# Decode attention: the K cache loaded in two transfers of 64 partitions, 32 KB to a partition

## The chip, the core and the metric

The kernel runs on one core of a Trainium2 chip. The metric is the device time of one execution in microseconds, the median of several runs. The core's engines are named as in the profile: PE (TensorE, matrix products), PEld (its weight loads), DVE (VectorE), ACT (ScalarE), POOL (GpSimd) and SP (SyncE, which issues most transfers here). Transfers between the chip's main memory and the core's on-chip memory run on 16 DMA engines. On-chip tiles have up to 128 partitions; a matmul's result goes to an accumulator memory (tiles with names in `_ps`).

## What is computed

One decode step for 8 sequences (B = 8, one token each, D = 512): attention over the last W = 2048 cached positions with 32 query heads on 8 cached heads (rep = 4) of Dh = 128, times the silu of a gated unit (F = 1792), added to x:

```python
xn = layernorm(x)
q = xn @ wq                                        # 32 heads of 128
k, v = the last 2048 positions of the caches       # 8 heads
p = softmax(q k^T * Dh**-0.5)
s = (p v) @ wo
h = sigmoid(xn @ w_gate) * (xn @ w_up)
out = x + s * silu(h @ w_down)
```

All inputs are bfloat16. The caches' windows are 33.55 MB each for K and V, wq and wo 4.19 MB each, gate, up and down 1.84 MB each: 81 MB that are read once.

## The kernel before, in words

**Loads.** Large tiles go through a ring of RING = 5 buffers of 128 partitions x 32 KB (`ring_tile`, L86). The list `loads` (L156) fixes their order: wq, K0, K1, K2, V0, then K3 V1, K4 V2, ... K7 V5, then V6, V7, gate and up, down, wo. `issue_loads` (L164) issues the next loads whenever a buffer is free (`free_bufs`); SP issues them all, in that order, on one queue. A buffer is free when its scores (`qk`, for a K) or its sums (`pv`, for a V) are done. A load's issue also waits until an earlier transfer that used the same one of eight completion semaphores has landed. Beside these, ACT loads x (`x_bf`, L84), and `load_x2` (L121) makes the copy of x that the last sum needs, x2, of two halves: POOL copies the first, and SP loads the second, 4 KB, between V1 and K4.

**Where K and V lie.** `load_heads` (L105) makes one transfer for a batch of K or V: each partition receives VC = 64 consecutive positions of two cached heads, that is two runs of 16 KB; partition 4p + gl holds positions 64p to 64p + 63 of the heads 2 gl and 2 gl + 1. The second index of the two is called gg.

**Setup.** POOL and DVE make constant tiles from an identity (L178 to L306), among them: SumM and Jneg, which spread the maximum over a group of rows and multiply it by the scale; Hm and quarter, masks over partitions; Cm4 and Cm2, masks for the sums; spr, for the spread; qz0 and qz1, zeroed here and filled with each batch's q by ACT. q is projected by PE (L316) when wq has landed.

**The loop over batches** (L614 to L652) is ordered by hand. In iteration b the DVE turns K of batch b in place, in blocks of 32 x 32 words (`k_turn`, four pieces n = 0 to 3 of 128 x 2048 words, L384), and between the pieces come the steps of the softmax for batch s = b - 1 and the sums for batch b - 3: `soft_max_part` (maximum of a row, L414, and a matmul with SumM, L420), `pv_rows` (L538), `soft_exp` (L424: one ACT exp that also sums), `soft_spread` (L438: a DVE transpose to pt_bf, 16 matmuls of 128 columns with spr to pc_ps, an ACT copy to pc_bf), `soft_den_part`, `soft_mask` (L475: four DVE multiplications by the columns of Hm that make pT). Then PE makes the scores of batch b in `qk` (L386): 32 matmuls of 32 output partitions x 512 columns into s_ps, for each of four words `we`, two gg and four gl. The half gg of the K tile lies in the pieces 2 gg and 2 gg + 1, so the matmuls of gg = 0 need only the first two pieces. Then PE makes `pv` (L491) of batch b - 2, 16 or 32 matmuls for each gg from pT and the V tile.

**The tail.** After the loop: `pv` and `pv_rows` for the last batches, the gated unit (`unit_in` to u_ps, L569; `unit_mid`, which makes hT; `unit_out` to b_ps, L599, and the gate), and 128 small matmuls with wo into a_ps (L676), which follow wo's pieces as they land. Two DVE operations on the result (prod, L690, and y, L694, which adds x2) and two stores end the kernel.

Of the kernel before, what the change touches and what calls it, by code (L numbers as in the profile page):

```python
# [10 lines left out]
def kernel(  # L11
# [13 lines left out]
    nc = tc.nc  # L25
    P = 128
    B, _, D = A_x.shape
    _, Hkv, Sk, Dh = A_k_cache.shape
    Hq = A_wq.shape[1] // Dh
    rep = Hq // Hkv  # L30
# [15 lines left out]
    NC16 = 16  # L46
    CL = VC // NC16
    GR = GL * rep
# [55 lines left out]

    def load_heads(t, cache, b):  # L105
        nc.sync.dma_start(
            out=t[:],
            in_=cache[b, :, win0:Sk, :].rearrange("h (p c) d -> p h (c d)", c=VC),
        )

    def load_k(b):
        t = ring_tile("k_sb")
        k_tiles[b] = t
        load_heads(t, A_k_cache, b)

    def load_v(b):
        t = ring_tile("v_sb")
        v_tiles[b] = t
        load_heads(t, A_v_cache, b)

    def load_x2():  # L121
        nc.gpsimd.tensor_copy(out=x2_sb[:B, :], in_=x_bf[:, :DC])
        nc.sync.dma_start(
            out=x2_sb[32 : 32 + B, :], in_=A_x.flatten_outer_dims()[:, DC:]
        )

# [30 lines left out]
    for b in range(3, B):  # L157
        loads += [(load_k, b), (load_v, b - 2)]
        if b == 3:
            loads.append((load_x2,))  # L160
    loads += [(load_v, B - 2), (load_v, B - 1), (load_in,), (load_down,), (load_wo,)]
    free_bufs = [RING]

    def issue_loads():  # L164
        while loads:
            small_one = loads[0][0] is load_x2
            if not small_one and free_bufs[0] == 0:
                return
            f, *a = loads.pop(0)
            f(*a)  # L170
            if not small_one:
                free_bufs[0] -= 1

    issue_loads()

    ident = consts.tile([P, P], bf16, name="ident")  # L178
    make_identity(nc, ident[:])
# [6 lines left out]
    nc.vector.bn_aggr(out=mv[:], in_=stats[:])  # L186
    eps_t = small.tile([B, 1], f32, name="eps_t")
    nc.vector.memset(eps_t[:], 1e-5)
    rstd = small.tile([B, 1], f32, name="rstd")
# [14 lines left out]
    for kt in range(KT):  # L204
        nc.tensor.transpose(
            out=xnT_ps[:, kt, :], in_=xn_bf[:B, kt::KT], identity=ident[:B, :B]
        )
    xnT_sb = work.tile([P, KT, PW], bf16, name="xnT_sb")
    nc.vector.memzero(xnT_sb[:])
    nc.vector.tensor_copy(out=xnT_sb[:, :, :B], in_=xnT_ps[:])  # L210
# [9 lines left out]
    for gg in range(NG):  # L220
# [9 lines left out]
        rows128.append(t)  # L230
    block = consts.tile([P, QP, PW], f32, name="block")
    quarter = consts.tile([P, QP], f32, name="quarter")
    nc.vector.tensor_reduce(
# [3 lines left out]
        op=ALU.add,  # L237
    )
    nc.gpsimd.tensor_copy(
        out=block[:], in_=quarter[:].unsqueeze(2).to_broadcast([P, QP, PW])  # L240
# [8 lines left out]
    SumM = consts.tile([P, P], f32, name="SumM")  # L249
    nc.vector.tensor_copy(  # L250
        out=SumM[:].rearrange("p (g j r) -> p g j r", j=QP, r=rep),
# [4 lines left out]
    )  # L256
    Jneg = consts.tile([P, QP], f32, name="Jneg")
    nc.vector.tensor_reduce(
        out=Jneg[:],
        in_=ident[:].rearrange("p (a j r) -> p j a r", j=QP, r=rep),  # L260
        axis=AX.XY,
        op=ALU.add,
    )
    nc.vector.tensor_scalar(
        out=Jneg[:], in0=Jneg[:], scalar1=-scale, scalar2=None, op0=ALU.mult
    )
    Hm = consts.tile([P, GL], f32, name="Hm")
    nc.vector.tensor_reduce(
        out=Hm[:],
        in_=ident[:].rearrange("p (a gl) -> p gl a", gl=GL),  # L270
        axis=AX.X,
        op=ALU.add,
# [8 lines left out]
    Cm2 = consts.tile([P, 2], f32, name="Cm2")  # L281
    nc.vector.tensor_reduce(
        out=Cm2[:],
        in_=ident[:].rearrange("p (u c x) -> p c u x", c=2, x=GR),
        axis=AX.XY,
        op=ALU.add,
    )
# [3 lines left out]
    )  # L291
    spr = consts.tile([P, CL, PW // GL, GL], bf16, name="spr")
    nc.gpsimd.tensor_copy(
        out=spr[:],
        in_=ident[:].rearrange("k (gl cl p) -> k cl p gl", gl=GL, cl=CL),
    )
    quad = consts.tile([P, QP, QP, PW], bf16, name="quad")
    for a in range(QP):
# [57 lines left out]
    def q_fill(b):  # L356
        z = qz[b % 2]
        for a in range(QP):
            rows = slice(PW * a, PW * (a + 1))
            for gg in range(NG):  # L360
                c0 = gg * QP * rep + rep * a
                nc.scalar.copy(  # L362
                    out=z[rows, GL * gg : GL * (gg + 1), :, c0 : c0 + rep],
                    in_=qc_sb[rows, :, gg, :, :, b].rearrange("p gl r we -> p gl we r"),
                )
# [20 lines left out]
    def qk(b):  # L386
        s_tiles[b] = psum.tile([P, W // QP], f32, name="s_ps")
        kv = k_tiles[b][:].rearrange(
            "p (g cl c wb i gl e) -> p g gl wb e c cl i",
            g=NG,  # L390
            cl=CL,
            c=NC16,
            wb=2,
            i=PH,
            gl=GL,
        )
        for we in range(WE):
            for gg in range(NG):
                for gl in range(GL):
                    h = GL * gg + gl  # L400
                    nc.tensor.matmul(  # L401
                        s_tiles[b][PW * gl : PW * (gl + 1), :],
                        lhsT=qz[b % 2][:, h, we, :],
                        rhs=kv[:, gg, gl, we // 2, we % 2],
                        start=(we == 0 and gg == 0),
                        stop=(we == WE - 1 and gg == NG - 1),
                        tile_position=(0, PW * gl),
                        skip_group_check=True,
                    )
        k_tiles.pop(b)  # L410

    def soft_max_part(b):
        mx = small.tile([P, 1], f32, name="mx")
        nc.vector.reduce_max(out=mx[:], in_=s_tiles[b][:], axis=AX.X)  # L414
        mj = small.tile([P, QP], f32, name="mj")
        nc.vector.tensor_scalar(
            out=mj[:], in0=Jneg[:], scalar1=mx[:], scalar2=None, op0=ALU.mult
        )
        mb_ps = psum1.tile([P, QP], f32, name="mb_ps", tag="misc")
        nc.tensor.matmul(mb_ps[:], lhsT=SumM[:], rhs=mj[:], start=True, stop=True)  # L420
        return mb_ps
# [16 lines left out]
    def soft_spread(b):  # L438
        p_bf = e_tiles[b][0]
        pt_bf = ppool.tile([P, NC16, NG, QP, rep], bf16, name="pt_bf")  # L440
        nc.vector.transpose(  # L441
            out=pt_bf[:].rearrange("p c g a r -> p (c g a r)"), in_=p_bf[:]
        )
        pc_ps = psum1.tile([P, CL, NC16, NG, rep], f32, name="pc_ps", tag="pc_ps")
        for cl in range(CL):
            for a in range(QP):
                nc.tensor.matmul(  # L447
                    pc_ps[PW * a : PW * (a + 1), cl],
                    lhsT=spr[:, cl].rearrange("k p gl -> k (p gl)"),
                    rhs=pt_bf[:, :, :, a, :],  # L450
                    start=True,
                    stop=True,
                    tile_position=(0, PW * a),
                    skip_group_check=True,
                )
        pc_bf = ppool.tile([P, VC, NG, rep], bf16, name="pc_bf")
        nc.scalar.copy(  # L457
            out=pc_bf[:].rearrange("p c g r -> p (c g r)"),
            in_=pc_ps[:].rearrange("p l c g r -> p (l c g r)"),
        )  # L460
        pc_tiles[b] = pc_bf
# [13 lines left out]
    def soft_mask(b, den_ps):  # L475
        rden = small.tile([P, 1], f32, name="rden", bufs=3)
        nc.vector.reciprocal(out=rden[:], in_=den_ps[:])
        rden_tiles[b] = rden
        pc = pc_tiles.pop(b)
        pT = ppool.tile([P, NG, VC, GL, rep], bf16, name="pT_sb")  # L480
        pT_tiles[b] = pT
        for gl in range(GL):
            nc.vector.tensor_scalar(  # L483
                out=pT[:, :, :, gl, :],
                in0=pc[:].rearrange("p c g r -> p g c r"),
                scalar1=Hm[:, gl : gl + 1],
                scalar2=None,
                op0=ALU.mult,
            )

    def pv(b, gg):  # L491
# [7 lines left out]
        for m in range(VC // nch):  # L499
            cg = m % ncg  # L500
            nc.tensor.matmul(  # L501
                o_ps[rows * cg : rows * (cg + 1), :],
                lhsT=pT_tiles[b][:, gg, nch * m : nch * (m + 1)].rearrange(
                    "p c g r -> p (c g r)"
                ),
                rhs=v[:, cols * m : cols * (m + 1)],
                start=(m < ncg),
                stop=(m >= VC // nch - ncg),
                tile_position=(0, rows * cg),
                skip_group_check=True,  # L510
            )
# [218 lines left out]
```

## Time and profile before

| | |
|---|---|
| median of 3 runs | 197.66 us (197.5 to 235.91) |
| profiled execution, time | 197.44 us |
| its span, first to last instruction | 195.7 us |
| PE busy | 111.6 us (57%) |
| DVE busy | 117.6 us (60%) |
| ACT busy | 38.6 us (20%) |
| POOL busy | 6.4 us (3%) |
| mean transfer rate over the span | 415 GB/s |
| mean granted PE clock | 0.813 of full speed |

How to read the profile's lines below. The page shows the span in 40 equal slices of 4.9 us: a digit is a busy share in tenths, GB/s is what the DMA engines moved, PEclk the granted clock. A line of a window has the window and its length, then busy time and number of instructions for PE, PEld, DVE, ACT and POOL, then granted clock, the mean busy share of the 16 DMA engines, and GB/s. A line of the transfers has the tile and its source, the issuing queue, how many, KB each and the median time in us from issue to landing. A line of the timeline has start and length in us, engine, line, operation, output <- inputs, shapes, count, and in brackets how long the engine sat idle before and what ended that.

### The profile page before, as it was taken

The page shows a single profiled execution, that of the slowest core. Times are in us where ns is not written, and L with a number is a line of the kernel's source. Part 1 is how long each engine was busy: PE and PEld are TensorE (multiplying, and loading weights), DVE is VectorE, ACT ScalarE, POOL GpSimd, SP SyncE. Part 2 cuts the span into 40 slices and gives each one's busy share as a digit, 9 for nine tenths or more (in the row PEclk, how much of TensorE's full clock was granted, in tenths as well). Part 3 has the DMA queues.
Part 4 walks back from the last instruction along what each step waited for, and adds up shares of the span by engine and source line. Part 5 has one row for each costly group of instructions (what it writes and reads, how often), then busy time and mean ns, then how long its engine had stood idle before and what let it go on. Part 6 is the DMA issues. An engine that isn't in the chain of part 4 may idle for free.

```text
span 195.7 us, 2620 instructions
## 1 busy us (share of the span) xinstructions
PE 111.6 (57%) x1092; PEld 44.6 (23%) x1092; DVE 117.6 (60%) x176; ACT 38.6 (20%) x112; POOL 6.4 (3%) x22
## 2 busy tenths in 40 slices
PE   0133025709809980799059914990796199684362
PEld 0011001102002240214022411150215024462351
DVE  3404498299299449935895489739936952455001
ACT  3001910015015011501141104211501110233000
POOL 2730000000000000000000000000000000000000
PEclk9999555966985996589757985699589669999998
DMA  6999999999999999999999999999999999999991
GB/s 241 457 408 442 432 429 429 429 432 425 429 429 429 427 429 429 432 424 439 432 439 422 439 435 435 429 432 425 432 429 429 425 429 429 429 431 429 416 396 41
DMA packets 6410, 81.17 MB, mean 415 GB/s; under 512 B 992, under 2 KB 1024, under 8 KB 1408
## 3 DMA queue, kind: packets, MB, share of 16 engines
q1 hardware_dynamic: 6368, 81.01, 97.2%
q8 instruction: 8, 0.13, 0.2%
q10 hardware_dynamic: 32, 0.01, 0.0%
q14 instruction: 2, 0.02, 0.0%
HBM read 81.01 MB, written 0.01 MB: 414 GB/s over the span
## 4 chain that ended last, share of the span: by engine, by line
PE 38%; DVE 35%; DMA 23%; ACT 1%; issue 1%; SPq 1%; DVEq 0%
PE s_ps L401 27%; DVE k_sb L384 27%; DMA wo_sb<-in_A_wo_dram 12%; DMA k_sb<-in_A_k_cache_dram 11%; PE o_ps L501 8%; DVE pt_bf L441 2%; DVE o_r L522 2%; PE o_ps L530 1%; DVE o_sb L552 1%; ACT o_r L518 1%; DVE o_q L543 1%; DVE mx L414 1%; PE a_ps L676 1%; SPq L147 0%; SPq L101 0%
## 5 line engine op out<-in xcount | busy, mean ns | idle before, releaser
L384 DVE STREAM_TRANSPOSE k_sb<-k_sb 128x2048 uint32<-128x2048 uint32 x32 | 72.9, 2291 | 5.7 <-DMA k_sb<-in_A_k_cache_dram 5.7
L401 PE MATMUL s_ps<-k_sb,qz 128*32 128x512 bf16 x256 | 61.6, 1086 | 11.8 <-DVE k_sb L384 11.5
L447 PE MATMUL pc_ps<-pt_bf,spr 128*32 128x128 bf16 x128 | 4.7, 292 | 40.7 <-DVE pt_bf L441 40.7
L414 DVE TENSOR_REDUCE mx<-s_ps 128x1 f32<-128x512 f32 x8 | 5.5, 691 | 29.0 <-PE s_ps L401 29.0
L501 PE MATMUL o_ps<-v_sb,pT_sb 128*32 128x256 bf16 (+1 forms) x416 | 21.0, 298 | 0.0
L401 PEld LDWEIGHTS <-qz 128*32 128x32 bf16 x256 | 8.8, 115 | 49.8 <-issue 49.7
L501 PEld LDWEIGHTS <-pT_sb 128*32 128x32 bf16 (+1 forms) x416 | 14.0, 101 | 14.5 <-issue 9.9
L362 ACT COPY qz<-qc_sb 32x64 bf16<-32x64 bf16 x64 | 16.4, 302 | 0.7
L518 ACT ACTIVATE o_r<-o_ps,Cm 128x128 f32<-128x128 f32 x16 | 5.9, 368 | 52.0 <-PE o_ps L501 52.0
L522 DVE SCALAR_TENSOR_TENSOR o_r<-o_ps,Cm,o_r 128x128 f32<-128x128 f32 x28 | 9.7, 350 | 9.8 <-ACT o_r L518 9.3
L428 ACT ACTIVATE p_bf<-s_ps,nm 128x512 bf16<-128x512 f32 x8 | 5.5, 687 | 49.7 <-DVE nm L425 49.7
L447 PEld LDWEIGHTS <-spr 128*32 128x32 bf16 x128 | 3.4, 121 | 41.4 <-issue 40.7
L530 PE MATMUL o_ps<-o_r,rows 128*128 128x128 f32 x32 | 7.5, 320 | 4.8 <-DVE o_r L522 4.8
L483 DVE TENSOR_SCALAR pT_sb<-pc_bf,Hm 128x512 bf16<-128x512 bf16 x32 | 9.0, 352 | 0.2 <-ACT pc_bf L457 0.2
L457 ACT CAST pc_bf<-pc_ps 128x512 bf16<-128x512 f32 x8 | 4.7, 586 | 20.3 <-PE pc_ps L447 20.3
L316 PE MATMUL q_ps<-wq_sb,xnT_sb 128*32 128x512 bf16 x32 | 3.8, 626 | 6.8 <-DMA wq_sb<-in_A_wq_dram 6.5
L676 PE MATMUL a_ps<-wo_sb,o_sb 128*32 128x128 bf16 x128 | 4.6, 219 | 3.9 <-DMA wo_sb<-in_A_wo_dram 3.9
L530 PEld LDWEIGHTS o_ps<-o_r,rows 128*128 128x128 f32 x32 | 4.8, 189 | 6.7 <-DVE o_r L522 6.7
L326 DVE CAST qx_sb<-q_ps 128x256 bf16<-128x256 f32 x4 | 1.5, 420 | 7.7 <-PE q_ps L316 7.7
L441 DVE STREAM_TRANSPOSE pt_bf<-p_bf 128x512 bf16<-128x512 bf16 x8 | 5.4, 675 | 0.9 <-ACT p_bf L428 0.9
L543 DVE SCALAR_TENSOR_TENSOR o_q<-o_ps,rden,block 128x128 f32<-128x128 f32 x8 | 2.8, 351 | 4.7 <-PE o_ps L530 4.7
L690 DVE TENSOR_TENSOR prod<-gate,a_ps 64x128 bf16<-64x128 f32 x2 | 0.5, 279 | 7.5 <-PE a_ps L676 7.5
(64 smaller groups left out, 56.2 us busy)
## 6 DMA issues: line engine op xcount, KB each, us to landing
k_sb<-in_A_k_cache_dram SPq DMA_DIRECT2D x8, 4096.0 KB, 29.9
v_sb<-in_A_v_cache_dram SPq DMA_DIRECT2D x8, 4096.0 KB, 23.4
wq_sb<-in_A_wq_dram SPq DMA_DIRECT2D x1, 3072.0 KB, 11.6
wgu_sb<-in_B_w_gate_dram SPq DMA_DIRECT2D x1, 1792.0 KB, 25.1
wgu_sb<-in_B_w_up_dram SPq DMA_DIRECT2D x1, 1792.0 KB, 28.9
wd_sb<-in_B_w_down_dram SPq DMA_DIRECT2D x1, 1792.0 KB
wo_sb<-in_A_wo_dram SPq DMA_DIRECT2D x1, 1408.0 KB
wq_sb<-in_A_wq_dram SPq DMA_DIRECT2D x1, 1024.0 KB
```

The lines of the kernel that those rows point to most:

```text
L362: nc.scalar.copy(out=z[rows, GL * gg : GL * (gg + 1), :, c0 : c0 + rep], in_=qc_sb[rows, :, gg, :, :, b].rearrange("p gl r we -> p gl we r"),)
L384: nc.vector.transpose(out=words, in_=words)
L401: nc.tensor.matmul(s_tiles[b][PW * gl : PW * (gl + 1), :], lhsT=qz[b % 2][:, h, we, :], rhs=kv[:, gg, gl, we // 2, we % 2], start=(we == 0 ...
L414: nc.vector.reduce_max(out=mx[:], in_=s_tiles[b][:], axis=AX.X)
L441: nc.vector.transpose(out=pt_bf[:].rearrange("p c g a r -> p (c g a r)"), in_=p_bf[:])
L447: nc.tensor.matmul(pc_ps[PW * a : PW * (a + 1), cl], lhsT=spr[:, cl].rearrange("k p gl -> k (p gl)"), rhs=pt_bf[:, :, :, a, :], start=True ...
L483: nc.vector.tensor_scalar(out=pT[:, :, :, gl, :], in0=pc[:].rearrange("p c g r -> p g c r"), scalar1=Hm[:, gl : gl + 1], scalar2=None, op0 ...
L501: nc.tensor.matmul(o_ps[rows * cg : rows * (cg + 1), :], lhsT=pT_tiles[b][:, gg, nch * m : nch * (m + 1)].rearrange("p c g r -> p (c g r)" ...
L518: nc.scalar.activation(out=o_r[:], in_=o_ps[:, 0:Dh], func=AF.Copy, scale=cm[:, 0:1])
L522: nc.vector.scalar_tensor_tensor(out=o_r[:], in0=o_ps[:, Dh * c : Dh * (c + 1)], scalar=cm[:, c : c + 1], in1=o_r[:], op0=ALU.mult, op1=AL ...
L530: nc.tensor.matmul(o2_ps[:], lhsT=rows128[gg][:].rearrange("p gl g r q -> p (gl g r q)"), rhs=o_r[:], start=(gg == 0), stop=(gg == NG - 1),)
L676: nc.tensor.matmul(a_ps[s][32 * c : 32 * (c + 1), :], lhsT=o2_sb[:, m, :], rhs=w_tiles["o"][:, m, DC * c + HC * s : DC * c + HC * (s + 1)] ...
```

## The change

- `load_k` no longer uses `load_heads`. It makes two transfers, one for each gg, each into 64 of the 128 partitions. Partition 64 gg + 4 q + gl receives KC = 128 consecutive positions, one run of 32 KB, of the head 2 gl + gg.
- `qk`: a partition's 128 positions are split into two halves ch, and a matmul reads, for one ch, columns of every one of the four turned pieces (cl is the outer index and a piece is one cl). There are as many matmuls of the same shape, and `q_fill` puts q in other places of qz, with as many copies.
- `soft_spread`: 8 matmuls of 256 columns for 16 of 128; spr is made of four copies on POOL instead of one. pc_bf has another order, so that `soft_mask` reads it contiguously and `pv` finds its columns of pT by (cl, gg, ch).
- `load_x2` is gone: POOL copies both halves of x from x_bf. The eps tile, the zeroing of xnT_sb, SumM and Cm2 move from DVE to POOL; Jneg's multiplication by the scale is done in the multiplication by the maximum; Hm is dropped for quarter.
- `load_heads` gets `parts`; V of the last batch is loaded by two transfers of 128 partitions, one for each gg.

The diff, cut:

```diff
-    CL = VC // NC16
+    KC = 2 * VC
+    CL = KC // (2 * NC16)
...
+    def load_heads(t, cache, b, parts=1):
+        src = cache[b, :, win0:Sk, :]
+        if parts == 1:
...
+        src = src.rearrange("(gl gg) (p c) d -> gg p gl (c d)", gg=NG, c=VC)
+        for gg in range(NG):
+            nc.sync.dma_start(
+                out=t[:, gg * VC * Dh : (gg + 1) * VC * Dh], in_=src[gg]
+            )
...
-        load_heads(t, A_k_cache, b)
+        src = A_k_cache[b, :, win0:Sk, :].rearrange(
+            "(gl gg) (q c) d -> gg q gl (c d)", gg=NG, c=KC
+        )
+        for gg in range(NG):
+            nc.sync.dma_start(out=t[P // NG * gg : P // NG * (gg + 1), :], in_=src[gg])
...
-        load_heads(t, A_v_cache, b)
-
-    def load_x2():
-        nc.gpsimd.tensor_copy(out=x2_sb[:B, :], in_=x_bf[:, :DC])
-        nc.sync.dma_start(
-            out=x2_sb[32 : 32 + B, :], in_=A_x.flatten_outer_dims()[:, DC:]
-        )
+        load_heads(t, A_v_cache, b, parts=NG if b == B - 1 else 1)
...
+    eps_t = consts.tile([B, 1], f32, name="eps_t")
+    nc.gpsimd.memset(eps_t[:], 1e-5)
+    xnT_sb = work.tile([P, KT, PW], bf16, name="xnT_sb")
+    nc.gpsimd.memset(xnT_sb[:], 0.0)
...
+    for c in range(NCOL):
+        nc.gpsimd.tensor_copy(
+            out=x2_sb[32 * c : 32 * c + B, :], in_=x_bf[:, DC * c : DC * (c + 1)]
+        )
...
-    nc.vector.tensor_copy(
+    nc.gpsimd.tensor_copy(
         out=SumM[:].rearrange("p (g j r) -> p g j r", j=QP, r=rep),
...
-    nc.vector.tensor_scalar(
-        out=Jneg[:], in0=Jneg[:], scalar1=-scale, scalar2=None, op0=ALU.mult
-    )
-    Hm = consts.tile([P, GL], f32, name="Hm")
...
+    nc.gpsimd.tensor_tensor(
+        out=Cm2[:], in0=Cm4[:, 0:2], in1=Cm4[:, 2:4], op=ALU.add
     )
...
-    spr = consts.tile([P, CL, PW // GL, GL], bf16, name="spr")
...
+    spr = consts.tile([P, CL // 2, 2, GL, 2, GL], bf16, name="spr")
+    order = ident[:].rearrange(
+        "k (gl u cl ih il) -> k cl ih il u gl", gl=GL, u=2, cl=CL // 2, ih=2
+    )
+    for cl in range(CL // 2):
+        for ih in range(2):
+            nc.gpsimd.tensor_copy(out=spr[:, cl, ih], in_=order[:, cl, ih])
...
-            for gg in range(NG):
-                c0 = gg * QP * rep + rep * a
+            gg, qh = divmod(a, 2)
+            for ch in range(2):
+                c0 = rep * (QP * gg + 2 * ch + qh)
...
         kv = k_tiles[b][:].rearrange(
-            "p (g cl c wb i gl e) -> p g gl wb e c cl i",
-            g=NG,
+            "p (cl ch c wb i gl e) -> p ch gl wb e c cl i",
+            ch=2,
...
-            for gg in range(NG):
+            for ch in range(2):
                 for gl in range(GL):
-                    h = GL * gg + gl
                     nc.tensor.matmul(
                         s_tiles[b][PW * gl : PW * (gl + 1), :],
-                        lhsT=qz[b % 2][:, h, we, :],
-                        rhs=kv[:, gg, gl, we // 2, we % 2],
+                        lhsT=qz[b % 2][:, GL * ch + gl, we, :],
+                        rhs=kv[:, ch, gl, we // 2, we % 2],
...
-            out=mj[:], in0=Jneg[:], scalar1=mx[:], scalar2=None, op0=ALU.mult
+            out=mj[:],
+            in0=Jm[:],
+            scalar1=mx[:],
+            scalar2=-scale,
+            op0=ALU.mult,
+            op1=ALU.mult,
...
-        for cl in range(CL):
+        pc_ps = psum1.tile([P, CL // 2, 2 * NG, NC16, rep], f32, name="pc_ps", tag="pc_ps")
+        for cl in range(CL // 2):
             for a in range(QP):
                 nc.tensor.matmul(
                     pc_ps[PW * a : PW * (a + 1), cl],
-                    lhsT=spr[:, cl].rearrange("k p gl -> k (p gl)"),
-                    rhs=pt_bf[:, :, :, a, :],
+                    lhsT=spr[:, cl, a % 2].rearrange("k i u gl -> k (i u gl)"),
+                    rhs=pt_bf[:, :, :, a // 2, :].rearrange("p c g r -> p g c r"),
...
             nc.vector.tensor_scalar(
-                out=pT[:, :, :, gl, :],
-                in0=pc[:].rearrange("p c g r -> p g c r"),
-                scalar1=Hm[:, gl : gl + 1],
+                out=pT[:, :, gl, :],
+                in0=pc[:],
+                scalar1=quarter[:, gl : gl + 1],
...
-                lhsT=pT_tiles[b][:, gg, nch * m : nch * (m + 1)].rearrange(
-                    "p c g r -> p (c g r)"
-                ),
+                lhsT=pT_tiles[b][:, gg, l // 2, l % 2, c0 : c0 + rows],
```

## The prediction

> **What bounds the kernel now.** I read the slices first, then the queue, the windows, the transfers, and last the order of the work in one batch and in the tail.
>
> ```profile
> PEclk9999555966985996589757985699589669999998
> DMA  6999999999999999999999999999999999999991
> GB/s 241 457 408 442 432 429 429 429 432 425 429 429 429 427 429 429 432 424 439 432 439 422 439 435 435 429 432 425 432 429 429 425 429 429 429 431 429 416 396 41
> ...
> q1 hardware_dynamic: 6368, 81.01, 97.2%
> ```
>
> The DMA line holds 9 from the second slice to the last but one, and the rate under it stays near 430 GB/s: 81.01 MB at 430 GB/s is 188.4 us of a span of 195.7. So the transfers are the bound. The windows give the same rate exactly, in their last two columns (share of the 16 engines, GB/s):
>
> ```profile
> 2.50:5.00 2.50, 0.00 (x0) 0.00 (x0) 1.88 (x6) 0.42 (x2) 0.00 (x0) 1.00 1.18 478
> ...
> 30.00:60.00 30.00, 17.03 (x100) 4.33 (x99) 22.18 (x22) 4.38 (x14) 0.00 (x0) 0.78 1.00 428
> 60.00:120.00 60.00, 39.41 (x247) 13.15 (x248) 41.74 (x63) 11.96 (x39) 0.00 (x0) 0.76 1.01 432
> ...
> 170.00:185.00 15.00, 8.80 (x182) 6.36 (x181) 6.42 (x17) 4.16 (x8) 0.00 (x0) 1.00 1.00 426
> 185.00:191.00 6.00, 3.32 (x100) 2.94 (x101) 0.00 (x0) 0.00 (x0) 0.00 (x0) 1.00 0.97 392
> ```
>
> From 30 to 120 us the caches come in (16 KB runs), from 170 to 185 weights (14 KB and up): 426 to 432 whatever the run. Only the small last pieces of wo drop to 392. What all these transfers share is 16 engines and 128 written partitions. The caches are 67 of the 81 MB:
>
> ```profile
> k_sb<-in_A_k_cache_dram SPq DMA_DIRECT2D x8, 4096.0 KB, 29.9
> v_sb<-in_A_v_cache_dram SPq DMA_DIRECT2D x8, 4096.0 KB, 23.4
> ```
>
> At 430 GB/s one of them (4.19 MB) takes 9.75 us. Their 23 to 30 us from issue to landing say that each stands behind two others: the queue never runs dry. The chain of waits nevertheless names PE and VectorE (38% and 35%), because the loop over batches takes about as long as its two transfers: 20.4 us (k_sb pieces at 74.43, 94.91 and 115.26 us) and later 17.8 against 19.5. In the loop the order matters:
>
> ```profile
> 27.06 1.12 PE L401 MATMUL s_ps<-k_sb,qz 128*32 128x512 bf16 x4 [8.26 <-DVE k_sb L384]
> ...
> 31.44 6.55 PE L401 MATMUL s_ps<-k_sb,qz 128*32 128x512 bf16 x28 [3.26 <-DVE k_sb L384]
> ```
>
> Four score matmuls run when two of the four turned pieces are there, the other 28 after the fourth. And in the tail:
>
> ```profile
> 182.43 1.71 PE L599 MATMUL b_ps<-wd_sb,hT_sb 128*32 128x256 bf16 x28 [3.33 <-DMA wd_sb<-in_B_w_down_dram]
> ...
> 191.32 1.33 PE L676 MATMUL a_ps<-wo_sb,o_sb 128*32 128x128 bf16 x28 [0.40 <-DMA wo_sb<-in_A_wo_dram]
> ```
>
> PE waits for wd, then for wo: the end is the last byte of wo (191.3 us) plus 4.4 us of sums and store. hT is ready at 180.8, so compute may be 1.6 us later before it shows.
>
> The profiled execution took 197.44 us, 1.74 more than its span; the median is 197.66, 0.2 above. I sum against 197.44.
>
> **The change, part by part.**
>
> *K in two transfers of 64 partitions.* Eight of the 4096 KB K transfers become sixteen of 2097 thousand bytes, each into half of the partitions. The trace holds no large transfer into fewer than 128, so the price has two ends. If the rate belongs to the 16 engines or to the reading side, 64 partitions also take 430 GB/s: 0. If it belongs to the written partitions (430 over 128 is 3.4 GB/s each), 64 take half of it. K's 33.55 MB cost 78.0 us at 430 and 155.3 at half of 432, the best long window: +77.3. The two halves do not make this up for each other: both are issued back to back on one queue in which all earlier transfers kept all 16 engines busy (share 1.00), so all 16 are in the first half together and then in the second.
>
> Which end is nearer? No run length and no source moves the rate, so the reading side is not it. Between engine and destination there is one row, a weak one: from 2.5 to 5 us, when the first bytes come, the engines show 478 GB/s at a share of 1.18, 11% over their steady rate, so that 26.9 GB/s (430 over 16) is not what an engine cannot exceed. (Overlapping records may also make that number.) I take the half-rate end, +77.3, and keep 0 for the range.
>
> [...]
>
> *Runs of 32 KB for 16 KB.* K's packets fall from 2048 to 1024. From 185 to 191 us the engines were busy 16 × 6 × 0.97 = 93 us for 2.35 MB, which at 26.9 GB/s take 87.5: 5.6 us for some 700 small packets, 8 ns each. 1024 fewer are 8 us over 16 engines: −0.5 at most. I take 0, as the weights' longer runs show no higher rate.
>
> *More issues on SP.* Nine more of 0.60 us, and the second half of K3 now waits for the first half of K0, eight transfers earlier (to 21.6 us in the slow case, against an issue at 16.02). Behind it on SP stand only later loads, and the queue holds two transfers at each issue. At the tightest, 129.24 us, 62.9 MB less V5's own 4.19 were issued and 54.8 moved: 3.9 MB, 9 us of cover. Cost 0; without that cover 0.6 us a batch.
>
> *Scores.* Each score matmul now reads columns of all four turned pieces (ch is the inner, cl the outer index), so the four early ones wait too: 4 × 6.6/28 = 0.94 us later per batch, 7.5 us over eight. In the slow case K lands every 29.2 us (19.4 + 9.75) against a loop of 20.4 + 0.9: hidden. If K is not slower, it stays under the 9 us of queued bytes in the loop (5.7 us by 129 us) but shows in the tail, below.
>
> *Spread.* 8 matmuls of 256 columns for 16 of 128: 0.61 us becomes 0.3 to 0.6, while VectorE turns the last piece (2.2 us): 0.
>
> *Masks.* pT is written from a contiguous pc: 4 × 352 ns, bounds 0.13 (rden, one column) to 0.69 each (mx, 512 columns). They run while PE does scores, and VectorE idles there until mx (29.0 us in total): 0.
>
> *Constants, eps, x.* VectorE loses six setup instructions, 1.14 us by their rows, all before q's second piece, for which PE waits until 12.80: 0. GpSimd gains about 2 us (SumM as heads 0.29, Cm2 0.24 as rows, three more spr copies at 0.29 as quad, one x copy 0.39, memsets 0.3) and makes its old x copy earlier, so its qz memset ends at about 12.7 for 10.28; ScalarE first writes qz at 19.79: hidden by 7 us. The 4 KB load of x goes, 0.53 us of SP: 0.
>
> *Last V in two transfers.* V7 lands near 168 us, before it is needed at 173.7: 0.
>
> Sum: 197.44 + 77.3 = 274.7; I say 274.5.
>
> **The rivals.**
>
> *C, not slower: the rate belongs to the engines.* For it: a share of 1.00 at every run length. Against: the 1.18. K costs nothing, and what is left is the 0.94 us a batch. hT comes 7.5 us later, at 188.3, b_ps is done at 190.0, and 128 wo matmuls (44 took 1.41 us, so 4.1) end at 194.1 instead of 192.4: 197.44 + 1.7 = 199.1. It decides where two transfers of 64 partitions land in 9.75 us. Without the four matmuls' loss, 196.9 to 197.4.
>
> *B, between: engines drift apart.* Where one of two engines that share a destination gets ahead by a half (4.9 us), they are in different halves from then on, and the loss is paid once: 197.44 + 4.9 = 202.3. A partial lead of x us saves x in each of 16 halves: with 1 us 258, so 202 to 258. For it: nothing holds the engines together but the issues, two transfers ahead. Against: steady slices of 425 to 435 show no engine held up by another, so nothing makes a lead.
>
> *D, faster.* Longer runs lift the whole rate to 439, the best late slice: K in 76.4 us, −1.6, and the loop's 0.9 would have to hide too: 195.8. Over 2% faster (under 193.7) needs 3.7 us, more than all K packets' overhead.
>
> *The change does not do what it says:* if the transfers were still split over all partitions, it is C.
>
> **How the numbers follow.** A 0.60 (258 to 280), B 0.13 (202 to 258), C 0.23 (196 to 201.5), D 0.04. The forecast is A's time, 274.5. A's own range is 262 to 279: below by a lead of under 1 us, above by 211 GB/s for the half (half of 422, the lowest late slice, +81). As C holds more than 2 in 10, the overall range reaches down to 198, within C, and leaves out 0.10 of C, D and 0.03 above 280. Over 2% from 197.66 (about what a measurement of this kernel can tell): slower is A and B, 0.73; within is C and most of D, 0.25; faster 0.02.
>
> **What would show it.** A: the slices fall to about 215 GB/s for 19 us per K and return to 430 for V; K's two halves land 9.7 us apart; VectorE's k_sb waits for DMA in most batches. C: all slices at 430, the first score matmul after the fourth piece, and idle before a_ps gone. B: slices that start at 215 and rise. I am wrong if two K halves land within 10 us of each other's start at full rate, or if spread or scores wait for something other than k_sb.

## The result, and the profile after

The changed kernel took 306.53 us in the median of 4 executions (302.82 to 309.83), the kernel before 197.61 beside it; its two lower executions, 303.74 and 302.82, give a ratio of 1.5349, 95% interval 1.5323 to 1.5375. It is 109 us slower where I forecast 77, for the most part by the mechanism that I forecast. Over all measurements, those below too, some of its executions took 279 to 285 us and others 303 to 310 us, while the kernel before stayed within 0.5 us of 197.5 in all the later ones.

The profiled execution took 309.83 us with a span of 307.5. First its slices, now 7.7 us each (busy share of the DMA engines in tenths, then GB/s), and its queue, from the page of the changed kernel:

```profile
DMA  8999999998999899999999998999999999980000
GB/s 313 370 205 205 205 205 205 209 226 311 407 205 205 330 356 206 204 369 322 226 192 390 324 209 183 394 303 209 198 369 437 428 428 430 422 336 23 0 2 1
...
q1 hardware_dynamic: 5472, 81.01, 89.5%
```

The engines are as busy as before, but while a K comes they move 205 GB/s, half of the old rate. V and the weights still come at 430 (slices 31 to 35, counted from 1). The same bytes take until about 277 us instead of 191. And then the second thing, which I did not forecast: four slices without transfers. They are PE's, as the groups (busy us, mean ns of one, idle before) and the timeline show. The groups after the change:

```profile
L379 DVE STREAM_TRANSPOSE k_sb<-k_sb 128x2048 uint32<-128x2048 uint32 x32 | 72.9, 2291 | 109.3 <-DMA k_sb<-in_A_k_cache_dram 109.3
L395 PE MATMUL s_ps<-k_sb,qz 128*32 128x512 bf16 x256 | 60.1, 1088 | 24.9 <-DVE k_sb L379 24.9
L504 PE MATMUL o_ps<-v_sb,pT_sb 128*32 128x256 bf16 (+1 forms) x416 | 73.2, 767 | 0.0
...
L677 PE MATMUL a_ps<-wo_sb,o_sb 128*32 128x128 bf16 x128 | 13.4, 484 | 0.0
```

The first three of these groups on the page of the kernel before:

```profile
L384 DVE STREAM_TRANSPOSE k_sb<-k_sb 128x2048 uint32<-128x2048 uint32 x32 | 72.9, 2291 | 5.7 <-DMA k_sb<-in_A_k_cache_dram 5.7
L401 PE MATMUL s_ps<-k_sb,qz 128*32 128x512 bf16 x256 | 61.6, 1086 | 11.8 <-DVE k_sb L384 11.5
...
L501 PE MATMUL o_ps<-v_sb,pT_sb 128*32 128x256 bf16 (+1 forms) x416 | 21.0, 298 | 0.0
```

And the end of the changed kernel's timeline:

```profile
285.82 5.62 PE L600 MATMUL b_ps<-wd_sb,hT_sb 128*32 128x256 bf16 x26
...
291.13 13.45 PE L677 MATMUL a_ps<-wo_sb,o_sb 128*32 128x128 bf16 x128
```

VectorE now waits for K 109.3 us in all (5.7 before). The 128 matmuls with wo, whose code and shapes are unchanged, run from 291.13 without a pause, 13.45 us for 128 or 105 ns each (the 484 ns of the group count each matmul from its own start to its own end, and they overlap); before, 44 of them took 1.41 us, 32 ns each. The sums with V take 73.2 us for 21.0; gate and up take 6.0 us for 1.9, down 5.9 for 1.7. So PE worked at about 0.3 of its speed in this execution. (The scores did not slow down, 1088 ns for 1086: whatever slowed the other matmuls did not limit them. This page has no row of granted clocks, so what slowed PE is not shown.)

### The profile page after: what moved, and what is told of

The parts are those of the page before. It is cut to its first block, busy times and chain, and to the rows that moved or that the text cites. A ratio compares the mean times of both kernels' runs of the same rounds, so it can differ in the third digit from the quotient of the medians.

```text
span 307.5 us, 2521 instructions
## 1 busy us (share of the span) xinstructions
PE 198.0 (64%) x1028; PEld 90.4 (29%) x1028; DVE 115.6 (38%) x170; ACT 38.5 (13%) x112; POOL 7.9 (3%) x30
## 2 busy tenths in 40 slices
DMA packets 5514, 81.17 MB, mean 264 GB/s; under 512 B 1128, under 2 KB 1152, under 8 KB 1536
## 4 chain that ended last, share of the span: by engine, by line
PE 37%; DVE 25%; another core or an unknown queue 19%; DMA 16%; SPq 1%; issue 1%; DVEq 0%
DVE k_sb L379 19%; DMA k_sb<-in_A_k_cache_dram 16%; PE o_ps L504 15%; PE s_ps L395 7%; PE o_ps L531 5%; PE a_ps L677 4%; PE u_ps L570 2%; PE b_ps L600 2%; DVE pT_sb L484 1%; DVE pt_bf L440 1%; PE mb_ps L419 1%; DVE mx L408 1%; DVE o_sb L553 1%; SPq L126 1%
## 5 line engine op out<-in xcount | busy, mean ns | idle before, releaser
L379 DVE STREAM_TRANSPOSE k_sb<-k_sb 128x2048 uint32<-128x2048 uint32 x32 | 72.9, 2291 | 109.3 <-DMA k_sb<-in_A_k_cache_dram 109.3
L395 PE MATMUL s_ps<-k_sb,qz 128*32 128x512 bf16 x256 | 60.1, 1088 | 24.9 <-DVE k_sb L379 24.9
L504 PE MATMUL o_ps<-v_sb,pT_sb 128*32 128x256 bf16 (+1 forms) x416 | 73.2, 767 | 0.0
L504 PEld LDWEIGHTS <-pT_sb 128*32 128x32 bf16 (+1 forms) x416 | 35.4, 198 | 38.0 <-issue 34.6
L446 PE MATMUL pc_ps<-pt_bf,spr 128*32 128x256 bf16 x64 | 7.1, 516 | 38.8 <-DVE pt_bf L440 38.8
L419 PE MATMUL mb_ps<-mj,SumM 128*128 128x4 f32 x16 | 6.1, 451 | 26.7 <-DVE mj L410 26.7
L419 PEld LDWEIGHTS mb_ps<-mj,SumM 128*128 128x128 f32 x16 | 5.4, 377 | 38.2 <-DVE mj L410 34.0
L531 PE MATMUL o_ps<-o_r,rows 128*128 128x128 f32 x32 | 16.1, 609 | 0.2 <-DVE o_r L523 0.2
L531 PEld LDWEIGHTS o_ps<-o_r,rows 128*128 128x128 f32 x32 | 12.6, 475 | 3.0 <-DVE o_r L523 1.5
L677 PE MATMUL a_ps<-wo_sb,o_sb 128*32 128x128 bf16 x128 | 13.4, 484 | 0.0
L677 PEld LDWEIGHTS <-o_sb 128*32 128x32 bf16 x128 | 11.9, 217 | 1.7 <-issue 0.3
L484 DVE TENSOR_SCALAR pT_sb<-pc_bf,quarter 128x512 bf16<-128x512 bf16 x32 | 8.9, 346 | 0.0
```

The costliest lines, as they stand in the source:

```text
L379: nc.vector.transpose(out=words, in_=words)
L395: nc.tensor.matmul(s_tiles[b][PW * gl : PW * (gl + 1), :], lhsT=qz[b % 2][:, GL * ch + gl, we, :], rhs=kv[:, ch, gl, we // 2, we % 2], sta ...
L446: nc.tensor.matmul(pc_ps[PW * a : PW * (a + 1), cl], lhsT=spr[:, cl, a % 2].rearrange("k i u gl -> k (i u gl)"), rhs=pt_bf[:, :, :, a // 2 ...
L484: nc.vector.tensor_scalar(out=pT[:, :, gl, :], in0=pc[:], scalar1=quarter[:, gl : gl + 1], scalar2=None, op0=ALU.mult,)
L504: nc.tensor.matmul(o_ps[rows * cg : rows * (cg + 1), :], lhsT=pT_tiles[b][:, gg, l // 2, l % 2, c0 : c0 + rows], rhs=v[:, cols * m : cols ...
L531: nc.tensor.matmul(o2_ps[:], lhsT=rows128[gg][:].rearrange("p gl g r q -> p (gl g r q)"), rhs=o_r[:], start=(gg == 0), stop=(gg == NG - 1),)
```

## The experiments

**Is it K's transfers alone, and all of them?** The first four ran on one chip. The changed kernel again:

> The changed kernel once more, for a second trace of it. Theory D (K's transfers into 64 partitions run at 205 GB/s where others run at 430, and this is 33.55 MB / 0.205 - 78 = +86 us; the rest of the loss, 20 us, is a tail in which PE works at a quarter of its speed): about 303 us, slices at 205 GB/s while K comes, last byte of wo near 275 us, and wo's matmuls again some 100 ns each after it. Rival S (the rest of the loss belongs to the new scores, spread and sums themselves): the same time, but PE's matmuls of unchanged shape (wo, gate, up, down) as fast as before, 32 to 60 ns each, and the loss in the loop.

It took 281.24 us, so both forecasts of about 303 us missed. K came at 210 GB/s, as in Theory D, but the tail was as before the change: the last matmuls with wo start at 274.64 us, 4.4 us before the end of the span, and PE has its old speed, 44 of them in 1.41 us:

```profile
269.22 1.41 PE L677 MATMUL a_ps<-wo_sb,o_sb 128*32 128x128 bf16 x44 [0.41 <-ACT sigb L610]
```

The next run has one line back:

```diff
-        for gg in range(NG):
-            nc.sync.dma_start(out=t[P // NG * gg : P // NG * (gg + 1), :], in_=src[gg])
+        load_heads(t, A_k_cache, b)
```

> The changed kernel with one line back: K is loaded by the one transfer of 128 partitions and two 16 KB runs, as before, all else changed (K's rows lie elsewhere than the new scores take them to be, so the result is of mixed rows; the work is the same). Theory D: the whole loss is gone and what stays is my case C, 199.1 us (197 to 200), PE's unchanged matmuls as fast as before. Rival S: a large part of the loss stays, 215 us or more.

It took 199.88 us, ratio 1.0114 (1.006 to 1.0168): my case C, 199.1. All of the rest of the change costs 2.3 us, and K's two transfers the remaining 80 and more. Its windows (the last two columns are DMA share and GB/s) and its tail:

```profile
30.00:60.00 30.00, 16.87 (x78) 3.90 (x78) 20.38 (x21) 4.07 (x13) 0.00 (x0) 0.79 1.00 429
60.00:120.00 60.00, 39.95 (x240) 14.36 (x240) 38.92 (x62) 11.34 (x37) 0.00 (x0) 0.76 1.01 431
```

```profile
31.30 7.37 PE L391 MATMUL s_ps<-k_sb,qz 128*32 128x512 bf16 x32 [12.22 <-DVE k_sb L375]
...
190.72 3.74 PE L673 MATMUL a_ps<-wo_sb,o_sb 128*32 128x128 bf16 x128
```

All 32 score matmuls now start after the fourth piece, and PE no longer waits for wo, 128 matmuls in one go: the 0.94 us a batch has eaten the tail's slack, as worked out in C.

The reverse, the kernel before with `load_k` of the change:

> The kernel before with only K's transfers changed: two of 64 partitions with 32 KB runs (scores and spread as before, so the result is of mixed rows). Theory D: 300 us within 8, slices at 205 GB/s, wo's matmuls slow again. Rival S: 275 to 285 us, that is the transfers' 86 us alone.

It took 291.5 us, between the two forecasts, with wo's matmuls 41 ns each (5.2 us for 128). K's transfers alone make the kernel before slow. The 10 us over the changed kernel beside it lie in K's landings, which from K3 on come 31 to 34 us apart where the changed kernel's come 30 us apart (K7 at 233.96 us for 224.10); why they spread, one execution does not say.

**Half of the partitions, or which half?** K in three transfers, the first into the middle:

```diff
-        for gg in range(NG):
-            nc.sync.dma_start(out=t[P // NG * gg : P // NG * (gg + 1), :], in_=src[gg])
+        nc.sync.dma_start(out=t[32:96, :], in_=src[0])
+        nc.sync.dma_start(out=t[0:32, :], in_=src[1][0:8])
+        nc.sync.dma_start(out=t[96:128, :], in_=src[1][8:16])
```

> The changed kernel with the same 32 KB runs of K in three transfers: partitions 32 to 95 (64 of them), 0 to 31, and 96 to 127 (the result is of mixed rows). [...] Rival N (what counts is how many partitions a transfer writes): 64 partitions at 205 GB/s wherever they lie and 32 at 103: K costs 10 + 20 us a batch, total over 370 us.

It took 257.67 us, far below N's 370. Its slices (6.4 us each) swing between above 400 and 180 to 230:

```profile
GB/s 288 451 415 323 225 410 348 179 328 364 177 369 225 233 218 410 406 213 239 435 438 261 218 410 456 246 297 435 433 310 215 399 431 314 245 420 412 238 206 46
```

What can be read from them cleanly is the start, when wq has landed and V0 is not yet issued (it is at 22.55 us). The five microseconds in which K0's first transfer comes, first here, into partitions 32 to 95, then in a run of the changed kernel (its 285.43 us are below), into 0 to 63:

```profile
12.50:17.50 5.00, 3.18 (x28) 1.06 (x27) 2.37 (x5) 0.00 (x0) 1.69 (x2) 1.00 0.97 419
```

```profile
12.50:17.50 5.00, 3.18 (x28) 1.03 (x27) 1.71 (x5) 0.00 (x0) 1.71 (x2) 1.00 1.08 223
```

Both read the same bytes in the same 32 KB runs into 64 partitions, at 419 and at 223 GB/s. So it is neither the number of partitions, nor the bytes in a run, nor the reading side, but which partitions are written. The rest of this run says less. K1 lands 19.7 us after K0 (52.42 and 32.71), where 64 partitions at 430 GB/s and twice 32 at 205 would make 15 by my estimate (4.9 and twice 5.1), and K costs 58 us more than in the kernel with K in 128 partitions, not the 43 of that estimate. The two transfers of 32 partitions have sources with 8 outer blocks, like the extra transfer further down, whose packet count speaks for 8 engines; so half of the engines probably had no work in them and ran ahead, which is inferred: from 12 to 70 us 18.1 MB came, 5.5 MB more than K0 to K2, which landed by 69.8 us, hold.

Then came the 32 KB runs into all 128 partitions in one transfer, and the two halves on two queues:

```diff
-        for gg in range(NG):
-            nc.sync.dma_start(out=t[P // NG * gg : P // NG * (gg + 1), :], in_=src[gg])
+        nc.sync.dma_start(out=t[:], in_=A_k_cache[b, :, win0:Sk, :].rearrange("h (q c) d -> q h (c d)", c=KC))
```

> The changed kernel with K in one transfer of 128 partitions, each with one 32 KB run as in the change (16 positions' blocks by 8 heads, so the result is of mixed rows). Theory P (the loss comes of writing half of the partitions at a time): as the kernel with K in 128 partitions, 198 to 201 us, K at 430 GB/s. Rival R (the 32 KB run itself is slow): 275 to 285 us, slices near 210 GB/s.

```diff
-            nc.sync.dma_start(out=t[P // NG * gg : P // NG * (gg + 1), :], in_=src[gg])
+            (nc.sync, nc.gpsimd)[gg].dma_start(out=t[P // NG * gg : P // NG * (gg + 1), :], in_=src[gg])
```

> The changed kernel with the same two transfers of each K, the second half issued by GpSimd's queue instead of SP's, so that halves of both kinds can be under way at once. [...] Rival N (a limit on a transfer into 64 partitions that does not depend on where they lie, or queues that take turns for whole transfers): 275 to 285 us.

Both missed. One transfer into all 128 partitions took 311.09 us, and two queues 299.13. The slices of the first, then of the second:

```profile
GB/s 334 345 203 203 203 203 229 208 233 303 381 203 203 324 345 204 207 318 348 208 203 328 322 208 199 309 320 214 195 267 386 379 360 434 257 146 423 292 31 16
```

```profile
GB/s 266 297 257 307 212 216 212 212 212 212 176 434 304 212 240 256 268 345 210 331 278 218 210 368 307 214 234 359 313 205 379 366 382 439 421 312 420 246 52 25
```

My theory as I had put it, half of the partitions at a time, fell: 128 partitions show the same 203 GB/s. Rival R's rate came out (its time did not, with K's landings up to 43 us apart), but R cannot be right either, since 32 KB runs came at 419 GB/s into partitions 32 to 95. What the slow ones have in common must be finer. This source has 16 outer blocks of 8 rows, V's has 32 of 4 pairs, so an engine may well serve 8 neighbouring partitions here; no trace shows which engine writes which partition. The 203, 223 and 419 GB/s led me to a guess, theory L: *what counts is the place that each engine writes at the same moment; where two write the same, each has half of its rate.* Which partitions make up one place, no run shows. L can be tested without touching a K transfer's form, by making half of the engines late.

**A head start.** One extra transfer between wq and K0, of 0.5 MB, whose source has 8 outer blocks, so that at most 8 engines should have work: its run has 8 packets of under 512 B more (1136 for 1128), where each K transfer more has 16 (1128 with K in two, 1000 in one), so I take it that 8 engines served it. With it and without, K's halves are also exchanged (`reversed(range(NG))`). The three ran on one chip:

```diff
...
+        nc.sync.dma_start(
+            out=k_tiles[2][:, 0:2048],
+            in_=A_v_cache[0, :, win0 : win0 + 256, :].rearrange("h (j c) d -> h j (c d)", c=16),
+        )
```

> The changed kernel with two edits: partitions 64 to 127 of each K are loaded before 0 to 63, and between wq and the first K there is one extra transfer of 0.5 MB whose source has 8 outer blocks, so that at most 8 of the 16 engines have work in it (64 KB each; it lands where K2 is written later, so the result is the reference's). Theory L (the limit is that all 16 engines write the same half at the same moment, two to one place; engines 0 to 7 serve partitions 0 to 63 in V's transfers and have the extra work): engines 0 to 7 run 5 us behind 8 to 15, which then are always in the other half, in K and beside V: K at 400 GB/s or more, 203 to 225 us in all. Rival T (each transfer into a half has its own limit of 210 GB/s, whatever the others do): 280 to 290 us.

> The same extra transfer, K's halves in the order of the change. Theory L: engines 8 to 15 are ahead as well, but now into the half that 0 to 7 are writing with V (V on 0 to 63 beside K's first half on 0 to 63), so that the collisions only move: 275 to 295 us. Rival T: 280 to 290 us too; a time near 210 us would mean that the head start alone does it and that L's map of V is wrong.

> The changed kernel with K's halves in the other order and no extra transfer. Theory L: all engines still in step, 279 to 292 us. Rival T: the same. It shows what the order alone is worth.

They took 277.46, 302.14 and 306.11 us, all three outside the ranges of L and of T. What they do show is a sign: with both edits 29 us less than with the order alone, while the head start alone stays above 300 us (the changed kernel itself was not run beside them). The landings told why the gain was small: K1 came 14.8 us after K0 with the extra transfer and 20.1 without. Two halves at twice 4.88 us less the lead, 14.8 us, make a lead of 2.4 us, not 5; that is what 64 KB on each of 8 engines take at 27 GB/s (430 over 16). So the transfer was doubled to 1 MB (`0:4096`, 512 positions, `c=32`), with the changed kernel and the exchanged halves beside it on the same chip:

> As the kernel with head start and order, the extra transfer twice as long (1 MB, 128 KB on each of 8 engines). With 0.5 MB the second K landed 14.9 us after the first instead of 20.1, which by L (a half costs twice 4.9 us less the lead) is a lead of 2.4 us, just what 64 KB take at 27 GB/s. Theory L: 128 KB give a lead of 4.9 us, a whole half: K1 lands about 10 us after K0, K runs near 430 GB/s beside V as well, and the total is 205 to 235 us. Rival T: no better than with 0.5 MB, 275 to 290 us.

> The same extra transfer of 1 MB with the halves in the order of the change. Theory L: K1 also lands about 10 us after K0 (in K0 to K2 the two groups of engines are in opposite halves in either order), but from the first V on they collide, V against the first half of K, and the gain is lost: 255 to 300 us. If the order does not matter, as with the other one, L's account of V is wrong.

> The changed kernel again, as the measure for these runs on the same chip. Theory L: periods between K's landings of 29.7 us that stay even give 280 us; periods that grow from batch to batch, as where the halves were exchanged (32 to 40 us), give 300 us or more.

> The changed kernel with K's halves in the other order, again. If the chip is what made 306 us of it, this and the changed kernel beside it differ by less than 5 us; if the order is, by 20 or more.

| edit | us |
|---|---|
| 1 MB head start and exchanged halves | 220.21 |
| 1 MB head start | 285.56 |
| neither (the changed kernel) | 285.43 |
| exchanged halves | 299.31 |

With the exchanged halves the extra megabyte makes the changed kernel 65 us faster; neither edit does it alone. Both times that L had given came true. The other two runs lie between their signs: 285.43 us with landings 30.0 to 32.1 us apart, and 14 us between the two orders, where less than 5 or 20 and more had been the alternatives. The timeline of the first shows K0 and K1 landing 10.2 us apart; the changed kernel's, below it, 20.0:

```profile
36.10 8.89 DVE L388 STREAM_TRANSPOSE k_sb<-k_sb 128x2048 uint32<-128x2048 uint32 x4 [17.71 <-DMA k_sb<-in_A_k_cache_dram]
46.34 2.31 DVE L388 STREAM_TRANSPOSE k_sb<-k_sb 128x2048 uint32<-128x2048 uint32 x1 [1.34 <-DMA k_sb<-in_A_k_cache_dram]
```

```profile
33.39 8.89 DVE L379 STREAM_TRANSPOSE k_sb<-k_sb 128x2048 uint32<-128x2048 uint32 x4 [14.84 <-DMA k_sb<-in_A_k_cache_dram]
53.36 2.31 DVE L379 STREAM_TRANSPOSE k_sb<-k_sb 128x2048 uint32<-128x2048 uint32 x1 [11.09 <-DMA k_sb<-in_A_k_cache_dram]
```

With the head start alone K0 and K1 also land 10.3 us apart (36.13 and 46.45); the loss comes with the first V. The windows show it: first with both edits, then with the head start alone, then the changed kernel.

```profile
20.00:60.00 40.00, 8.99 (x44) 2.15 (x45) 18.60 (x12) 6.91 (x23) 0.00 (x0) 0.94 0.99 385
60.00:120.00 60.00, 35.91 (x208) 11.54 (x211) 41.19 (x58) 12.20 (x42) 0.00 (x0) 0.76 1.00 409
120.00:150.00 30.00, 22.05 (x171) 7.88 (x170) 18.41 (x28) 5.35 (x18) 0.00 (x0) 0.83 1.02 414
```

```profile
20.00:60.00 40.00, 9.13 (x44) 2.83 (x45) 18.43 (x12) 7.01 (x23) 0.00 (x0) 0.94 1.00 334
60.00:120.00 60.00, 34.00 (x188) 9.70 (x187) 27.64 (x40) 10.12 (x35) 0.00 (x0) 0.73 1.00 283
120.00:150.00 30.00, 14.40 (x80) 5.58 (x80) 14.10 (x21) 3.76 (x13) 0.00 (x0) 0.60 1.01 264
```

```profile
20.00:60.00 40.00, 8.04 (x34) 1.98 (x35) 15.49 (x10) 6.38 (x20) 0.00 (x0) 0.92 1.00 210
60.00:120.00 60.00, 25.78 (x142) 9.22 (x145) 30.41 (x42) 9.73 (x33) 0.00 (x0) 0.67 1.00 279
120.00:150.00 30.00, 14.72 (x88) 5.44 (x83) 14.15 (x22) 4.17 (x14) 0.00 (x0) 0.73 1.00 278
```

This is as L has it, except that beside V it had K near 430 GB/s and the rows have 409 and 414. By L, with engines 8 to 15 half a K ahead, the two groups are in opposite halves of K. Beside V, L takes engines 0 to 7 to write partitions 0 to 63, which no trace shows; if those ahead are then at K's partitions 64 to 127, nothing meets, and if they are at 0 to 63, two meet again. What the runs show is that the same transfers come at 210 or at 385 to 414 GB/s, depending on a lead of some engines and on the order of the halves; that two engines meet at one place is inferred. The share of the engines is 0.99 to 1.02 in all nine rows, at 210 GB/s as at 414, so it does not tell these rates apart.

The 1 MB head start with exchanged halves, and the changed kernel, in four executions each:

> The kernel with the 1 MB extra transfer and the exchanged halves, timed in rounds beside the changed kernel. Theory L: 216 to 226 us in every execution, 60 us or more under the changed kernel of the same call. Rival: the 220 us were chance, since nothing holds the engines apart: executions between 220 and 290 us.

> The changed kernel, timed in rounds once more, for the 303 to 310 us of its first measurement. Theory D': the transfers alone give 279 to 286 us, and where it is 300 us or more PE's matmuls of the tail take some 100 ns (a quarter of their speed) or K's landings lie 32 us apart and more. Rival: 303 us with matmuls of 30 ns and landings 29.7 us apart, which would leave the first measurement unexplained.

The first took 221.19 us (219.04 to 222.52), ratio 1.1131 (1.1072 to 1.1191) to the kernel before, so its 220 us were not chance. The second gave 284.52, 305.17, 303.95 and 281.07. The profiled one, 284.52 us, has wo's matmuls at 41 ns. Of the two above 300 us there is no profile; the granted clocks recorded for them, 0.685 and 0.728, lie near those of the other two (0.755 and 0.706). An earlier set on another chip was steady:

> The changed kernel, timed in rounds beside the kernel before, for how far its time varies between executions. Theory D (transfers set the time, K at 210 GB/s): 279 to 283 us in every execution in which PE's wo matmuls take about 30 ns each, and 300 to 310 us where they take 100 ns. Rival: steady at about 303 us with fast wo matmuls.

It took 279.99 us (278.93 to 281.21), ratio 1.4194 (1.4137 to 1.425), K's landings 29.3 to 29.7 us apart from K2 on. The 6 us between its profiled execution (279.15) and the one of 285.43 us are in the landings: K7 lands at 221.8 and at 228.4 us. Why the changed kernel takes more than 300 us in some executions stays open. The one profile of such an execution, 309.83 us, has the same landings as that of 285.43 us (K7 at 228.9 us for 228.4) and 24 us of slow PE, most of them after the last byte. That the others are slow for the same reason is not shown: the three beside it have granted clocks of 0.726 to 0.74 on record, as have the executions with a fast PE. Nor is it the only way there: with the halves exchanged it was 306.11 and 299.31 us with wo's matmuls as fast as before, and there the landings lie further and further apart, from 31 and 32 us up to 38 and 40.

**The small edits alone,** in the kernel before (x by GpSimd, moved constants, folded scale, no Hm, last V in two):

> The kernel before with the small edits alone: x for the last sum by GpSimd, constants and memsets moved, Jneg's scale folded, Hm dropped, the last V in two transfers; K, scores, spread and the order of pc as before. My sum has all of these at 0 (work in the setup's or the loop's slack): 197.3 to 197.8 us, the same. Rival: the removed VectorE work or the earlier last V is worth something, 196.5 us or less.

It took 197.49 us, ratio 1.0002 (0.9992 to 1.0011): nothing, in either direction. No version here beats the kernel before.

## Why the prediction was wrong, point by point

- **The bound** (transfers, 430 GB/s whatever the run) was right, and the run without K's new transfers keeps 429 to 431.
- **K in two transfers, +77.3:** the direction was right, the size a little low. K came at 205 to 212 GB/s where I took 216: the first K's landed 20.0 and 21 us apart where I had 19.4, and all of K at these rates costs 80 to 86 us. Against the 199.9 us of the kernel with only that undone, it is 80 us (279.99) to 86 (285.43). That 64 partitions take half of the rate was an estimate (430 over 128), which no row of the profile before showed.
- **The written partitions' number as what sets the rate (64 take half)** was too coarse: 64 partitions in the middle came at 419 GB/s, 128 in one transfer at 203. That the half rate comes of two engines writing one place at one moment can explain these runs and is inferred from them; which partitions share a place was not shown.
- **The first step that failed: "The two halves do not make this up for each other ... all 16 are in the first half together", with an upper end of 280.** They came at half rate from the start, as said. But that all engines then stay in step was my assumption, which no run shows, and I priced a lead only as a gain (B: "a partial lead of x us saves x"). What a lead does depends on where it leads: with the halves exchanged, the one made here saves 65 us (220.21 for 285.43), and in the order of the change nothing (285.56). Without a made lead the landings of one and the same kernel come 29.7 us apart in one execution and 30 to 32 in another, which took it from 279.15 to 285.43 us, over my upper end. That engines drift apart there is argued, not seen.
- **The second step that failed, and the larger: the tail was taken over unchanged,** 4.4 us after the last byte. In the profiled execution it was 30 us, because PE's unchanged matmuls took 3 times as long. Of the 35 us between my sum and that execution (309.83 and 274.7), some 8 are the last byte's (about 277 for 268.6) and 26 the tail's. I had costed PE's unchanged work by the rows of one profile in which it hardly ever waits. Why PE was slow is open, and so is whether it was slow in the other three executions of that measurement, which have no profile.
- **Scores, +0.94 us a batch, hidden if K is slow and 1.7 us if not:** right. Without the slow K the kernel is 2.3 us slower, and the start of the 32 matmuls and of wo's show it.
- **Runs of 32 KB, 0:** no run shows a gain by them, and none has them at the full rate in 128 partitions, so the term was not measured by itself.
- **Constants, eps, x, last V, each 0:** right, 1.0002 together. **Spread and masks, 0:** these were not in that run; they are part of the 2.3 us, of which C's 1.7 are the scores. Masks took 346 ns for 352. The spread's 8 matmuls of 256 columns took 0.62 us, as long as the 16 of 128 before, where I had 0.3 to 0.6.
- **Rivals:** C is the run with K in 128 partitions, 199.9 for 199.1. B's lead exists, but had to be made here (that two engines share a destination, as B has it, was not shown), and it paid in one order of the halves only; with it the time was 220 us where B had 202.3. D did not occur.

## What to carry to other kernels

When transfers are the bound, ask for each of them which partitions it writes and in what company, and not only how many partitions and bytes it has: 64 partitions took 419 GB/s where they were 32 to 95 and 223 where they were 0 to 63. 16 busy engines had a share of 1.00 here at 210 GB/s and at 409, so read GB/s beside the share. The same transfers came at 210 or at 385 to 414 GB/s with the order of the halves and with a lead of some engines; test that by making some engines late. And where a change leaves an engine waiting, do not take it for certain that its unchanged work lasts as long as in the old profile: here it took 3 times as long in one execution and the same in others.

## What the runs showed that I had not expected

- One extra transfer of 1 MB at the start, together with the other order of K's halves, made a kernel that moves 81 MB faster by 65 us (285.43 to 220.21); it still came at 414 GB/s from 120 to 150 us, so what it set up lasted.
- The order of K's two halves, which changes no byte, cost 14 us (285.43 and 299.31 on one chip, one execution each).
- Two queues did not help: 299.13 us, with slices at 212 GB/s while both had halves to load. That the engines change between the queues in step would explain it; it was not shown.
- PE ran the same matmuls at 105 and at 32 ns in two executions of the same program.
